# Sliding-window attention and RWKV channel mix: the first batch's q and k in half quads, its mask on PE, and batch 3's outputs turned by the crossbar

## The chip, the core and the metric

The kernel runs on one core of a Trainium2 chip. A core has TensorE (PE), VectorE (DVE), ScalarE (ACT), GpSimd (POOL) and SyncE (SP), each with its own in-order queue, and 16 DMA engines. SP and ACT issue transfers on hardware queues, POOL on a software queue that can also convert fp32 to bf16 on the way. The metric is the device time of one execution in microseconds (us), less is better.

## What is computed

```python
B, H, S, D = 8, 8, 576, 64; window = 128; scale = 1 / sqrt(D)
scores = scale * q @ k^T - slope[h] * (i - j)        # only 0 <= i - j < 128, else -1e9
attn = softmax(scores);  x = (attn @ v) as [B, S, H*D = 512]
x_prev = x shifted by one row of the sequence (zeros first)
xk = mu_k * x + (1 - mu_k) * x_prev;  xr = the same with mu_r
k = relu(xk @ w_k)            # 512 -> 1024
out = sigmoid(xr @ w_r) * ((k * k) @ w_v)             # 1024 -> 512
```

All inputs and the output are fp32 in DRAM. The kernel computes in bf16 with fp32 accumulation; the first half of the mix's gate is a tanh, with the factor folded into the relu.

## The kernel before

The kernel is a list of steps. Each step (`op`, `dma`, `pool_op`) names its engines, an estimated duration, the steps it depends on, a priority, and the buffers it takes and gives back (`Hold`). `Plan.run` simulates the engines with these estimates and so writes out a fixed order of instructions for each engine; the chip then runs these orders with semaphores between engines. A step's priority comes from `rank`, which adds the constants of `LEAD`, `SHIFT` and `NUDGE` (a number for each step by its index). A step that may run on two engines goes to one of them by the plan. All transfers of POOL are issued in the order of `LOADS` and then batch by batch.

Names of the trace: `qx` holds fp32 q and k of the first loads, `raw` q and k as loaded, `qt` and `qk` q and k with the head dimension on partitions, `at` the exponentials, `vs` and `tv` v with a column of ones, `xu` the normalised output of attention, `xt` that output transposed, `dl`, `xk`, `xr` the shift and its two mixes, `kk` the squared relu, `rs` the gate, `ot` the result. `duo` are two pairs of PSUM banks, `uno` four single ones.

*Batches 1 to 7.* Heads come in two quads of 4. `quad_load` (L559) brings a quad's q or k (576 rows) with 18 rows of 64 in each partition, 32 partitions a head. `turn` (L1145) transposes it on DVE (L1150), in 32 x 32 blocks, into `qt`. `scores4` (L1160) computes four heads at once, each on 32 rows of PE (two passes for 64), in two halves: `QUAD0` (k blocks 0 and 1 with q rows 0 to 384) and `QUAD1` (the rest), each 512 columns a head. ACT takes the exponentials of two heads at a time (L1190), and DVE multiplies them by a mask that holds the bias's exponential and the window (L1200). `attend` multiplies with v (L796) and normalises on DVE (L802, L807). `out_t` transposes on PE (L834) and copies on ACT (L710) for batches 1 to 3; for batches 4 to 7 (`XO`) `out_flip` uses a transposing DMA from SP (L882). `shift` makes xk and xr on DVE (L860, L867). `gate_load` puts a one-row copy on POOL's queue (L653) ahead of a batch's loads, for batches 6 and 7, that waits for the transposing DMAs of the batch two before.

*Batch 0* has a path of its own. Its rows 0 to 256 are loaded in fp32 by SP (q) and ACT (k), eight transfers of 128 KB (L574): two heads, two heads, then four. The first two pairs of heads are cast to bf16 on DVE and transposed on PE (L1091); the other two pairs are transposed in fp32 on PE (L1088). Copies by ACT or DVE put them into `qk`. Rows 256 to 512 come through POOL (L536) and are transposed on PE in 64 x 64 blocks (`qk_quad`, L1044), the last 64 rows apart (`tail_load` L554, `tails` L897). `scores` (two heads at a time on 64 rows of PE, L740) first writes the bias and the window by a matmul of scaled identity (`sid`) and distance (`dist`) into PSUM (L727), so that no mask is multiplied. Part 0 (rows 0 to 256) goes through to xk before part 1. The mask for the later batches is made by eight exponentials on ACT (L1130) that wait for part 0's last xk.

*Channel mix.* `channel_mix` takes a run of columns (256, 256, 384 and 256 columns for the first two batches, then 512, 384 and 256 for each pair): for each of 8 blocks four matmuls with w_k (L949), relu on ACT (L956), a square on ACT (L920) or DVE (L922); then for each 128 rows four matmuls with w_r (L967), tanh on ACT (L974), eight matmuls with w_v (L983), the product on DVE (L988) and a store by SP. Before the first data come, and in gaps, PE runs 90 matmuls on zeros (`warm`, L701).

POOL's order at the start is `LOADS = 'vK23tVkabRcWw'`: first half of batch 0's v, first half of w_k, run loads of rows 256 to 512 for the two quads, the tails, second half of v, second half of w_k, batch 1's q and k, w_r, batch 1's v, the halves of w_v.

```python
QUAD0 = (((0, 0, 256), (1, 128, 256)), 0)
QUAD1 = (((2, 256, 256), (3, 384, 192), (4, 512, 64)), 256)
PART = (((((0, 0, 256), (1, 128, 128)), 0),),
        ((((1, 256, 128), (2, 256, 256)), 128),
         (((3, 384, 128), (3, 512, 64), (4, 512, 64)), 512)))
```

Each triple is a block of 128 keys, the first query row and the number of queries.

Of the kernel before, what the change touches and what calls it, by code (L numbers as in the profile page):

```python
# [9 lines left out]
FP32 = mybir.dt.float32  # L10
# [172 lines left out]
def kernel(  # L183
# [30 lines left out]
    NQ, NA, NX, NV, NC, NT = 4, 4, 4, 2, 2, 3  # L214
    XO = range(4,B)
# [3 lines left out]
    NWARM = 90  # L219
    LOADS = 'vK23tVkabRcWw'  # L220
    XD = 4
    OTL = 3.5
    FIN = 384
    RATE = 284.0
    QUAD = 0.040
    RUN = {2: 64 * 284 / 345.0}
# [4 lines left out]
    FX = (0, 4, 4, 4, 4, 4, 0, 0)  # L231
# [3 lines left out]
    WAIT = 5.15  # L235
    COST = {'first': 1.28, 'v': 1.15, 'q': 0.944, 'ts': 0.66, 'tv': 0.58, 'w': 0.88, 'quad': 1.0, 'run2': 1.55, 'flip': 1.0, 'mu': 1.0, 'x': 1.0}

    def XU(b, g):
        return (DVE,)

    def SQ(order):
        return (DVE, ACT)

    XT0 = (ACT,)
    QK0 = (ACT, DVE)
    CAST = (DVE,)
    FT = (2, 3)
    KQ = ACT
    VCUT = True
    VDEP = 1  # L250
    TCOST = 1.5
    TURN = 0.42
    KLAST = 1

    def XT(b, g):
        return (ACT,) if b else XT0

# [3 lines left out]
    def many(n, shape, dtype, name):  # L261
# [5 lines left out]
    tv_buf = many(NV, [128, H, W], BF16, "tv")  # L267
    ts_buf = many(1, [128, H, D], BF16, "ts")
    tt_buf = many(1, [128, G, 3, 64], BF16, "tt")
    qk_buf = many(NQ, [128, 2, SM], BF16, "qk")  # L270
    qx_buf = cst.tile([128, 4096], BF16, name="qx")
    raw1 = raw_buf[1].rearrange("p i c x -> p (i c x)")
    half_buf = raw1[:, 0:4096].rearrange(
        "p (a i r h d) -> p a i r h d", a=2, i=2, r=2, d=D)
    part_buf = raw1[:, 2048:4096].rearrange(
        "p (i h r d) -> p i h r d", i=2, r=2, d=D)
    stage = qx_buf.bitcast(FP32).rearrange(
        "p (g i w) -> p g i w", i=2, g=4)
    at_buf = many(NA, [128, 2 * 1024 + 64], BF16, "at")
    rc_buf = many(NX, [128, 2, NJ], FP32, "rc")  # L280
# [12 lines left out]
    dist = cst.tile([128, 768], BF16, name="dist")  # L293
    sid = cst.tile([128, H, 128], BF16, name="sid")
    wk_sb = cst.tile([128, NPO, DF], BF16, name="wk_sb")
# [19 lines left out]
    plan = Plan(dict(p2=2, p1=N1, pt=4 - N1, qk=NQ, at=NA, xu=NX, vs=NV, cb=NC, qt=NT, ts=1, tt=1, xt=2, dl=2, dl0=4,  # L315
# [10 lines left out]
    def dve_t(n, fast=1):  # L326
# [4 lines left out]
        PE: (379.11, 948.28, 321.48, 777.92, 344.48, 715.92, 627.75, 578.6, 241.8, 354.15),  # L331
        ACT: (700.83, 2.12, 322.35, 108.16, 185.72, -3.46, 340.58, 397.46, 747.05, 580.68),
        DVE: (282.18, -111.4, 162.81, 61.6, 37.49, 18.01, -37.8, -38.84, 70.95, -86.71),
# [3 lines left out]
        PE: {(0, 0): -1189.02, (3, 0): 492.42, (2, 0): 367.63, (1, 0): 298.05, (1, 1): -728.2, (1, 2): 117.95, ('p1', 'fxk'): -1.92, ('rl', 'fp1'): -1166.05, ('frl',): 219.95, ('rs', 'fp1'): 514.38, ('p1', 'fkk'): 4.9, ('fkk',): 426.5, ('ot', 'fp1', 'frs'): 532.6, ('fp1', 'frs'): -626.2},  # L337
        ACT: {(0, 0): -688.81, (3, 0): -610.15, (2, 0): -722.11, (1, 0): 289.16, (1, 1): -432.67, (1, 2): 1038.71, ('p1', 'fxk'): 478.01, ('rl', 'fp1'): 76.23, ('frl',): 491.94, ('rs', 'fp1'): -82.07, ('p1', 'fkk'): -497.1, ('fkk',): 342.85, ('ot', 'fp1', 'frs'): -48.3, ('fp1', 'frs'): 278.04},
# [123 lines left out]
    def dma(queue, kb, issue, emit, deps=(), need=(), free=(), lat=(1.0, 0.9), flip=False, kind='x'):  # L462
# [809 lines left out]
```

## Time and profile before

| | us |
|---|---|
| median of 3 runs | 228.2 (227.05 to 228.41) |
| the profiled execution | 227.53 |
| its span | 225.8 |
| PE, DVE, ACT, POOL busy | 217.1, 196.3, 166.6, 59.7 |

In the profile "L949" is line 949 of the kernel before. A row of a group reads: line, engine, operation, out<-in with shapes, count, then busy us and mean ns of one, then idle time of the engine before these instructions and what ended it. A row of a timeline reads: start, length (several merged instructions may stand in one row), engine, line, operation, count, and in brackets the idle time before. Ends of matmuls are modelled and overlap the next one's start, so what a matmul occupies is read from start to start. A row of the chain reads start, length, what. Granted clock 1.00 is full speed of TensorE.

### The profile page before, as it was taken

What the parts mean: (1) busy time and instruction counts of PE and PEld (TensorE: products, weight loads), DVE (VectorE), ACT (ScalarE), POOL (GpSimd) and SP (SyncE); (2) the same over time, 40 slices, a digit from 0 to 9 for tenths busy, and PEclk for the clock granted to TensorE, in tenths of its full rate; (3) what the DMA queues carried; (4) which work ended last, traced back from release to release, by engine and by line L of the source; (5) the groups of instructions that cost most, each with busy time, mean ns of one, the idle gap of its engine ahead of it and who ended that gap; (6) DMA issues with size and microseconds to landing.
All of it is one profiled execution on the core that took longest, in us unless ns stands there. A gap on an engine that the chain in (4) does not pass through costs nothing.

```text
span 225.8 us, 5825 instructions
## 1 busy us (share of the span) xinstructions
PE 217.1 (96%) x2339; PEld 128.5 (57%) x2339; DVE 196.3 (87%) x386; ACT 166.6 (74%) x311; POOL 59.7 (26%) x88
## 2 busy tenths in 40 slices
PE   8999978999999999999999999999999999999993
PEld 8576636755756555554774546445674455456542
DVE  7388999999999999999999999999989966983332
ACT  3669999766999789978996796677996684427511
POOL 8776525465100910160007500091000000000000
PEclk9999999999999999999999999999999999999998
DMA  6999999999971997095434995489991315140023
GB/s 157 182 165 195 202 153 207 192 175 233 208 162 49 83 197 179 3 130 88 151 77 58 219 190 108 106 130 188 165 112 29 144 46 121 39 154 37 3 93 139
DMA packets 66298, 29.74 MB, mean 132 GB/s; under 512 B 53976, under 2 KB 58336, under 8 KB 66272
## 3 DMA queue, kind: packets, MB, share of 16 engines
q0 software_dynamic: 46832, 16.26, 66.9%
q1 hardware_dynamic: 17696, 12.53, 20.5%
q10 hardware_dynamic: 1744, 0.59, 1.0%
q8 instruction: 18, 0.29, 0.5%
q14 instruction: 8, 0.07, 0.1%
HBM read 33.56 MB, written 9.44 MB: 190 GB/s over the span
## 4 chain that ended last, share of the span: by engine, by line
PE 80%; DVE 8%; ACT 6%; DMA 3%; issue 1%; SPq 1%; DVEq 0%; ACTq 0%
PE uno L949 25%; PE uno L983 25%; PE uno L967 12%; PE duo L796 7%; PE duo L1173 6%; DMA qx<-in_q_dram 3%; DVE xu L807 2%; DVE qt L1150 2%; ACT at L1190 2%; PE uno L834 2%; PE uno L701 1%; DVE xk L867 1%; ACT mask L1130 1%; ACT at L754 1%; DVE xr L867 1%
## 5 line engine op out<-in xcount | busy, mean ns | idle before, releaser
L949 PE MATMUL uno<-xk,wk_sb 128*128 128x256 bf16 (+2 forms) x416 | 71.3, 314 | 1.7 <-DVE xk L867 1.3
L983 PE MATMUL uno<-wv_sb,kk 128*128 128x512 bf16 (+2 forms) x296 | 68.4, 374 | 0.0
L1190 ACT ACTIVATE at<-duo 128x1024 bf16<-128x1024 f32 x56 | 55.3, 1038 | 12.5 <-PE duo L1173 12.3
L956 ACT ACTIVATE rl<-uno 128x256 bf16<-128x256 f32 (+2 forms) x104 | 47.7, 483 | 14.1 <-PE uno L949 12.8
L949 PEld LDWEIGHTS <-wk_sb 128*128 128x128 bf16 x416 | 38.6, 98 | 24.1 <-issue 3.0
L983 PEld LDWEIGHTS <-kk 128*128 128x128 bf16 x296 | 27.2, 98 | 30.1 <-issue 1.9
L540 POOL DMA_DIRECT2D vs<-in_v_dram x32 | 28.5, 903 | 38.9 <-PE duo L796 29.9
L1200 DVE TENSOR_TENSOR at<-at,mask 128x1024 bf16<-128x1024 bf16 x56 | 37.1, 679 | 1.0 <-ACT at L1190 1.0
L967 PE MATMUL uno<-wr_sb,xr 128*128 128x512 bf16 x144 | 35.9, 379 | 0.0
L974 ACT ACTIVATE rs<-uno 128x512 bf16<-128x512 f32 x36 | 22.0, 618 | 18.5 <-PE uno L967 17.5
L920 ACT ACTIVATE kk<-rl 128x256 bf16<-128x256 bf16 (+2 forms) x67 | 33.7, 530 | 0.8
L1150 DVE STREAM_TRANSPOSE qt<-raw 128x576 f32<-128x576 f32 x28 | 33.7, 1233 | 0.0
L988 DVE SCALAR_TENSOR_TENSOR ot<-rs,uno 128x512 f32<-128x512 bf16 (+2 forms) x37 | 24.0, 663 | 6.7 <-ACT rs L974 4.6
L867 DVE SCALAR_TENSOR_TENSOR xr<-dl,mu_sb,xt 128x576 bf16<-128x576 bf16 (+1 forms) x32 | 24.6, 774 | 0.1
L867 DVE SCALAR_TENSOR_TENSOR xk<-dl,mu_sb,xt 128x576 bf16<-128x576 bf16 (+1 forms) x32 | 24.5, 774 | 0.0
L807 DVE TENSOR_TENSOR xu<-duo,rc 128x640 bf16<-128x640 f32 x28 | 22.8, 818 | 1.5 <-PE uno L834 0.8
L796 PEld LDWEIGHTS <-at 128*128 128x128 bf16 x576 | 21.6, 98 | 4.4 <-issue 0.3
L967 PEld LDWEIGHTS <-xr 128*128 128x128 bf16 x144 | 13.4, 98 | 13.6 <-issue 0.2
L922 DVE TENSOR_TENSOR kk<-rl 128x256 bf16<-128x256 bf16 (+2 forms) x37 | 12.2, 334 | 8.7 <-ACT rl L956 8.0
L796 PE MATMUL duo<-vs,at 128*128 128x65 bf16 x448 | 18.9, 193 | 0.0
L1173 PE MATMUL duo<-qt 32*128 32x256 bf16 (+2 forms) x560 | 18.0, 250 | 0.7 <-ACT at L1190 0.4
L1173 PEld LDWEIGHTS <-qt 32*128 32x128 bf16 x560 | 11.9, 92 | 11.5 <-issue 9.7
(73 smaller groups left out, 160.4 us busy)
## 6 DMA issues: line engine op xcount, KB each, us to landing
out_dram<-ot SPq DMA_DIRECT2D x34, 256.0 KB, 2.8
vs<-in_v_dram POOLq DMA_DIRECT2D x32, 128.0 KB, 10.0
raw<-in_q_dram POOLq DMA_DIRECT2D x14, 288.0 KB, 8.2
raw<-in_k_dram POOLq DMA_DIRECT2D x14, 288.0 KB, 9.3
wk_sb<-in_moe_w_k_dram POOLq DMA_DIRECT2D x2, 512.0 KB, 7.5
wv_sb<-in_moe_w_v_dram POOLq DMA_DIRECT2D x2, 512.0 KB, 11.5
qx<-in_k_dram ACTq DMA_DIRECT2D x4, 128.0 KB, 5.1
qx<-in_q_dram SPq DMA_DIRECT2D x4, 128.0 KB, 4.8
```

The lines of the kernel that those rows point to most:

```text
L540: return dma(POOL, 256, issue_t(1024), lambda e: nc.gpsimd.dma_start(out=vs_buf[h.idx][:, j, :, 0:D], in_=v[b, :, 128 * j:128 * j + 128].r ...
L796: nc.tensor.matmul(a[:, hl, t - t0], lhsT=at[:, lo:lo + 128], rhs=vs[:, u, 2 * g + hl, :] if u < NF else tvb[:, 2 * g + hl], start=(u == u ...
L867: lambda e: nc.vector.scalar_tensor_tensor(out=buf[hk.idx][:, g, e0 + c0:e0 + c1], in0=dls(), scalar=mu[:, g:g + 1], in1=xc(1), op0=ALU.mu ...
L920: nc.scalar.activation(out=out, in_=in_, func=AF.Square)
L949: nc.tensor.matmul(one(hp)[:, 0:n], lhsT=wk_sb[:, po, 128 * fo:128 * fo + 128], rhs=xk_buf[hx.idx][:, po, c0:c1], start=(po == 0), stop=(p ...
L956: a = op(ACT, act_t(n), [s], pr, lambda e, hp=hp, hr=hr: nc.scalar.activation(out=rl_buf[hr.idx][:, 0:n], in_=one(hp)[:, 0:n], func=AF.Rel ...
L967: nc.tensor.matmul(one(hp), lhsT=xr_buf[hx.idx][:, po, 128 * c:128 * c + 128], rhs=wr_sb[:, po], start=(po == 0), stop=(po == NPO - 1))
L983: nc.tensor.matmul(one(hv)[:, a:b], lhsT=kk_buf[hk.idx][:, fo, o:o + 128], rhs=wv_sb[:, fo, a:b], start=(fo == 0), stop=(fo == NFO - 1))
L1150: nc.vector.transpose(out=qt_buf[hq.idx][:, S * i:S * i + S].rearrange("p s t -> p (s t)").bitcast(FP32) .rearrange("p (q t) -> p t q", t=TB),
L1173: nc.tensor.matmul(two(hps[j // 2])[:, j % 2, c0:c0 + n], lhsT=qt[r:r + 32, S + 128 * u:S + 128 * u + 128, t], rhs=qt[r:r + 32, q0:q0 + n, t],
L1190: lambda e, ah=ah, j=j: nc.scalar.activation(out=ah(), in_=two(hps[j]), func=AF.Exp, scale=float(scale)), (), [hps[j]])
L1200: nc.vector.tensor_tensor(out=a, in0=a, in1=m, op=ALU.mult)
```

## The change

Batch 0 uses the quads' path of the other batches, in two halves of rows.

- The first half of each quad (k rows 0 to 256, q rows 0 to 384: what `QUAD0` needs) is loaded in fp32 in one transfer each, k by SP and q by ACT, into two `kk` buffers; a cast on ACT or DVE writes it as bf16 into `raw`. The rest (k 256 to 576, q 384 to 576) comes by POOL with conversion, four transfers.
- DVE transposes each half (`turn_half`), `scores4` computes it on 32 rows of PE. Bias and window of all four half scores of batch 0, and of the first half of quad 0 of batch 1, are written on PE (`emit_b`); those exponentials have no mask multiplication. The second quad's first half uses four single PSUM banks and four exponentials of 512 columns.
- The run loads, the tails, PE transposes of q and k with their copies, `scores`, and the wider part of `dist` are gone.
- The mask's exponentials wait for the fourth cast, in place of part 0's last xk.
- POOL's order: v, w_k first half, half loads, w_k second half, second half of v, batch 1's q and k, w_r, batch 1's v, w_v.
- Batch 3 joins batches 4 to 7 in the transposing DMA, and batch 5's loads get the gate.
- Squares of the first mix are on DVE alone; the normalising of batch 0's second part may go to ACT. Warm-up matmuls are 36. Buffers: `at` 5 (4), `vs` and `tv` 3 (2), `qt` 4 (3), `rc` 6 (4).
- `LEAD` is zero, `SHIFT` empty, `NUDGE` another table, `WAIT` 0: the order of all engines is a new one.

```diff
-    NQ, NA, NX, NV, NC, NT = 4, 4, 4, 2, 2, 3
-    XO = range(4,B)
+    NA, NX, NV, NC, NT = 5, 4, 3, 2, 4
+    XO = range(3,B)
...
-    NWARM = 90
-    LOADS = 'vK23tVkabRcWw'
+    NWARM = 36
+    LOADS = 'idvK34kVaRbcWw'
...
+    BIAS = ((0, 0, 0), (0, 0, 1), (0, 1, 0), (0, 1, 1), (1, 0, 0))
+    SINGLE = ((1, 0),)
...
-    FX = (0, 4, 4, 4, 4, 4, 0, 0)
+    FX = (0, 1, 1, 1, 1, 1, 0, 0)
...
     def XU(b, g):
+        if b == 0:
+            return (DVE, ACT)
         return (DVE,)
 
     def SQ(order):
-        return (DVE, ACT)
+        return (DVE, ACT) if order else (DVE,)
...
+    CAST = (ACT, DVE)
+    CUT = ((0, 384, 576), (0, 256, 576))
...
+    def half_load(i, c, t, h, g):
+        t0, r = CUT[i][t], CUT[i][t + 1] - CUT[i][t]
+        src = (q, k)[i][0, 4 * c:4 * c + 4, t0:t0 + r].rearrange("h (p r) d -> h p r d", p=32)
+        e0, e1 = t0 // 32 * D, (t0 + r) // 32 * D
+        return dma(POOL, HALFKB[r], issue_t(128), lambda e: nc.gpsimd.dma_start(
+            out=raw_buf[h.idx][:, i, c, e0:e1].rearrange("p (r d) -> p r d", d=D), in_=src), [g], kind="half")
...
+        for c in range(2):
+            for i in (1, 0):
+                r = CUT[i][1]
+                src = (q, k)[i][0, 4 * c:4 * c + 4, 0:r].rearrange("h (p r) d -> h p (r d)", p=32)
+                eng, e = (SPE, nc.sync) if i else (ACT, nc.scalar)
+                x = dma(eng, r * 1.024 * HWCOST, 0.46, lambda _, i=i, c=c, e=e, src=src: e.dma_start(
+                    out=stage(c, i), in_=src), [last["kk0"]], lat=(0.85, 0.75), kind="first")
+                cl[0][c, i, 0] = op(CAST, {ACT: act_t(r * 2, True), DVE: dve_t(r * 2)}, [x],
+                                    (0, 0, 0, 2 * c, 5), lambda e, i=i, c=c, r=r: copy_any(
+                    e, raw_buf[ch[0].idx][:, i, c, 0:2 * r], stage(c, i)), (), [hs[c]])
...
-    ms = [op(ACT, act_t(256, True), [n_dist] + gate, (2, h), lambda e, h=h: make_mask(h))
+    ms = [op(ACT, act_t(256, True), [n_dist, n_cast[3]], (2, h), lambda e, h=h: make_mask(h))
           for h in range(H)]
...
+        def emit_b(e):
+            for j in range(4):
+                for (u, q0, n) in pieces:
+                    c0 = BASE[u] + q0 - 128 * u - a0
+                    nc.tensor.matmul(
+                        bank(j)[:, c0:c0 + n], lhsT=sid[:, 4 * c + j],
+                        rhs=dist[:, 0:n], start=(u == pieces[0][0]), stop=False,
+                        skip_group_check=True)
...
-                            start=(t == 0), stop=(t == 1), skip_group_check=True)
+                            start=(t == 0 and not bias), stop=(t == 1), skip_group_check=True)
...
+            if bias:
+                res[p].append(x)
+                continue
...
+    def turn_half(c, t, hq, deps):
+
+        res, n = [], None
+        for i in (1, 0):
+            t0, w = CUT[i][t], CUT[i][t + 1] - CUT[i][t]
+
+            def emit(e, i=i, t0=t0, w=w):
+                nc.vector.transpose(
+                    out=qt_buf[hq.idx][:, S * i + t0:S * i + t0 + w].rearrange("p s t -> p (s t)")
+                    .bitcast(FP32).rearrange("p (q t) -> p t q", t=w // 32),
+                    in_=raw_buf[ch[0].idx][:, i, c, 2 * t0:2 * (t0 + w)].bitcast(FP32).rearrange(
+                        "p (t w) -> p t w", w=32))
...
+    for c in range(2):
+        hq = Hold("qt")
+        y = turn_half(c, 0, hq, [])
+        has = [Hold("at"), Hold("at")]
+        s0, m0 = scores4(0, c, 0, hq, has, y)
+        first.append((hq, y, has, s0, m0))
+        for j in range(2):
+            g = 2 * c + j
+            prio = (0, 0, 0, g)
+            r, hx = attend(0, g, 0, 2, has[j], m0[j] + vl[0][0:2], prio)
+            xks[0, 0, g], xrs[0, 0, g] = out_t(0, g, 0, 2, hx, [r], prio, xh[0], xth[0], late)
```

More of the change, by code (lines that the diff above doesn't have):

```diff
@@ new lines @@
+    s0.succ.append((n_mut, 0.0))
+    y[1].succ.append((n_mcopy[0], 0.0))
+    for n in (n_mut, n_mcopy[0]):
+        n.left += 1
+    for f in late:
+        xrs[0, 0, f.g] = f([xks[0, 0, G - 1]])
+    for c, (hq, y, has, s0, m0) in enumerate(first):
+        y = turn_half(c, 1, hq, [(x, 0.0) for x in y])
+        s1, m1 = scores4(0, c, 1, hq, has, y + [(s0, 0.0)])
+        for j in range(2):
+            g = 2 * c + j
+            prio = (0, 0, 1, g)
+            r, hx = attend(0, g, 2, NJ, has[j], m0[j] + m1[j] + vl[0] + blank, prio)
+            xks[0, 1, g], xrs[0, 1, g] = out_t(0, g, 2, NJ, hx, [r], prio, xh[0], xth[0])
```

409 lines of the change are left out of this document (106 added, 303 removed), and 143 rows, old and new, of the table NUDGE.

## The prediction

> **What bounds the kernel now.** I read the page's totals and slices first, then the table of stretches, then the chain in order of time, then the timelines of PE, DVE and ACT over the first 40 us.
>
> ```profile
> span 225.8 us, 5825 instructions
> ...
> PE 217.1 (96%) x2339; PEld 128.5 (57%) x2339; DVE 196.3 (87%) x386; ACT 166.6 (74%) x311; POOL 59.7 (26%) x88
> ...
> DVE  7388999999999999999999999999989966983332
> ...
> PE 80%; DVE 8%; ACT 6%; DMA 3%; issue 1%; SPq 1%; DVEq 0%; ACTq 0%
> ```
>
> PE is the bound as a whole, and DVE runs beside it nearly full until three quarters of the span. The stretches (us; then busy time of PE, PEld, DVE, ACT, POOL with counts; granted clock; DMA share; GB/s) show where this is not so:
>
> ```profile
> 17.00:27.00 10.00, 10.00 (x176) 6.85 (x174) 8.96 (x24) 9.91 (x26) 6.19 (x8) 1.00 1.25 199
> 27.00:36.00 9.00, 6.31 (x99) 3.83 (x100) 9.00 (x19) 8.66 (x16) 3.34 (x6) 1.00 2.06 170
> 36.00:60.00 24.00, 23.46 (x281) 15.24 (x274) 23.67 (x41) 19.14 (x41) 12.31 (x18) 1.00 1.58 203
> ...
> 100.00:140.00 40.00, 40.00 (x427) 22.74 (x425) 38.93 (x65) 33.70 (x60) 7.49 (x10) 1.00 0.83 128
> ```
>
> From 36 us on PE has almost no gap and DVE has 1.07 us free in 40. Before that three things change places: up to 17 us PE waits for data, from 17 to 27 PE and ACT are both full, and from 27 to 36 PE is idle 2.7 us (9.00 - 6.31) while DVE has not a moment free. The chain in order of time (start, length, what) says what the first 17 us are made of, and two PE lines where the first stage of the channel mix begins:
>
> ```profile
> 2.27 5.85 DMA qx<-in_q_dram
> ...
> 8.16 1.12 PE uno L1088 x7
> ...
> 15.29 1.19 ACT qk L710 x4
> 16.48 0.62 ACT mask L1130 x2
> ```
> ```profile
> 16.64 1.03 PE L949 MATMUL uno<-xk,wk_sb 128*128 128x256 bf16 x8 [0.37 <-DVE xk L867]
> ...
> 34.69 0.92 PE L949 MATMUL uno<-xk,wk_sb 128*128 128x256 bf16 x7 [0.41 <-DVE xk L867]
> ```
>
> So the last q of the first loads lands at 8.12 us (2.27 + 5.85), real mix work starts at 16.64, and at 34.69 PE still waits for DVE's xk of batch 0. After 36 us a saved us of PE work is worth a us only if DVE follows.
>
> **The change part by part.**
>
> *First loads (until the first mix).* Before, eight transfers of 128 KB bring 1.05 MB as 256 and 512 byte runs. After, four transfers bring 4 heads x 64 x 4 bytes x (256 + 384) rows x 2 quads = 1.31 MB in runs of 2 and 3 KB, k by SP and q by ACT. Their speed is not in this trace; the rows around it, us by us:
>
> ```profile
> 2.00:3.00 1.00, 1.00 (x13) 1.00 (x11) 1.00 (x9) 0.10 (x1) 1.00 (x2) 1.00 0.91 268
> 3.00:4.00 1.00, 1.00 (x12) 1.00 (x11) 1.00 (x6) 1.00 (x1) 1.00 (x2) 1.00 1.03 287
> ...
> 7.00:8.00 1.00, 0.61 (x7) 0.26 (x6) 0.24 (x4) 1.00 (x2) 1.00 (x3) 1.00 1.92 160
> ```
>
> At 287 GB/s, 1.31 MB from 2.0 us land at 6.6, 1.5 us earlier than 8.12; if the time per byte stays that of before, (8.12 - 2.0) x 1.25 = 7.65, they land at 9.65, 1.5 later. What follows also changes: fp32 transposes on PE (1.12 us) and a copy make room for casts on ACT or DVE and stream transposes on DVE. Rows for these:
>
> ```profile
> L1200 DVE TENSOR_TENSOR at<-at,mask 128x1024 bf16<-128x1024 bf16 x56 | 37.1, 679 | 1.0 <-ACT at L1190 1.0
> L1150 DVE STREAM_TRANSPOSE qt<-raw 128x576 f32<-128x576 f32 x28 | 33.7, 1233 | 0.0
> ...
> L922 DVE TENSOR_TENSOR kk<-rl 128x256 bf16<-128x256 bf16 x19 | 5.5, 288 | 2.5 <-ACT rl L956 2.0
> ...
> L807 DVE TENSOR_TENSOR xu<-uno,rc 128x384 bf16<-128x384 f32 x4 | 2.2, 553 | 0.0
> ...
> L710 DVE COPY qk<-uno 128x256 bf16<-128x256 bf16 x4 | 1.5, 416 | 0.0
> ...
> L710 DVE CAST tt<-uno 128x256 bf16<-128x256 f32 x2 | 0.8, 418 | 0.0
> L710 DVE CAST qk<-uno 128x512 bf16<-128x512 f32 x1 | 0.7, 692 | 1.7 <-PE uno L1088 1.7
> ```
>
> A quad's first half costs one cast after its last landing (0.7 to 1.0 us) and DVE transposes of 256 + 384 of 576 columns, 640/576 x 1.23 = 1.4 us. That is about 0.9 us more than the PE transposes and copy (1.12 + 0.69 = 1.8 against some 2.3 plus a wait), and the first quad's half is already through while the second lands. I take 0 for this part; bounds -1.5 (early landing) and +2.5 (late landing 1.5 and 1.0 of longer chain).
>
> *Batch 0 on PE, second part.* Removed from 15 to 26 us: 64 transposes of 64 rows (L1044), 12 pairs of bias and 64-row score matmuls with the tails (L727, L740, L897). Measured start to start on PE's timeline:
>
> ```profile
> 17.97 0.50 PE L727 MATMUL duo<-dist,sid 128*128 128x384 bf16 x2
> 18.40 0.34 PE L740 MATMUL duo<-qk 64*128 64x128 bf16 x4
> 18.67 0.34 PE L1044 MATMUL uno<-ident,raw 64*64 64x64 bf16 x16
> 18.95 0.61 PE L949 MATMUL uno<-xk,wk_sb 128*128 128x256 bf16 x4
> 19.39 0.38 PE L727 MATMUL duo<-dist,sid 128*128 128x256 bf16 x2
> ...
> 35.84 0.64 PE L1173 MATMUL duo<-qt 32*128 32x256 bf16 x24 [0.23 <-ACT at L1190]
> 36.41 1.48 PE L949 MATMUL uno<-xk,wk_sb 128*128 128x256 bf16 x12
> ```
>
> A wide bias pair and its scores take 0.43 + 0.27, a narrow one with tails about 0.32 + 0.22 by the same reading (some 0.11 per 256 columns), 16 transposes 0.28: four of each is 4 x 0.70 + 4 x 0.54 + 4 x 0.28 = 6.1 us. Added: two half scores of 32 rows at 0.57 (36.41 - 35.84) = 1.1, and two bias sets of 4 x 512 columns, 8 x 0.11 plus 0.1 for the switch, 2.0 in all. PE saves 3.0 us here, and pays 1.0 for the bias of batch 1's first half. Net 2.0.
>
> *ACT and DVE from 17 to 36 us.* PE's saving is covered by the other two engines, so these decide. ACT: the 8 mask exponentials (they stood at 16.3 to 22 and cost 0.31 each start to start, 0.62 for two) now wait only for a cast and can lie in ACT's idle first 15 us: -2.5; its squares of the first mix go to DVE, its qk copies (1.19 for four) are gone. ACT stops being a limit. DVE: -4 x 0.416 = -1.7 for qk copies, -0.8 for tt, +2.2 for four half transposes (320 + 192 columns, twice: 1024/576 x 1.233), +1.2 for four more squares (4 x 0.288; I count half of the eight as already there), -1.4 for two mask multiplications of batch 1 (2 x 0.679); xu of the second part may go to ACT, 0 to -2.2 (4 x 0.553). Sum -0.5 to -2.7. DVE was busy 8.96 + 9.00 = 17.96 of these 19 us, so the stretch can shrink to 17.5 or 15.3: 1.5 to 3.7 us. PE allows it: 10.00 + 6.31 - 2.0 = 14.3. I take 2.0, near the lower end, as moving xu is only an option and DVE also has to wait for its inputs.
>
> *Loads by GpSimd.* Four half loads replace four run loads and two tail loads, and the second half of wk goes ahead of v's second half. The queue was the pace for batch 1, whose last k is what GpSimd's next issue waited for:
>
> ```profile
> 27.53 0.74 POOL L565 DMA_DIRECT2D wv_sb<-in_moe_w_v_dram  x1 [0.59 <-DMA raw<-in_k_dram]
> ```
>
> It carries 4 x 128 + 2 x 64 = 640 KB before and 512 after, so batch 1 lands some 0.8 us earlier (128 KB of its own at 170 GB/s), and v's second half about as late as before or up to 3 us later, behind 512 KB more. I price both at 0: the attention that needs v is paced by DVE. If v is later than DVE, it costs up to 3.
>
> *Batch 3 by the crossbar.* Removed: 20 PE transposes and 4 ACT copies. Added: 4 issues on SP, ahead of output stores, and a gate on POOL ahead of batch 5's loads.
>
> ```profile
> 46.16 0.72 PE L834 MATMUL uno<-ident,xu 128*128 128x128 bf16 x10
> 46.72 1.03 PE L983 MATMUL uno<-wv_sb,kk 128*128 128x512 bf16 x4
> ...
> L710 ACT COPY xt<-uno 128x576 bf16<-128x576 bf16 x12 | 7.8, 661 | 1.5 <-PE uno L834 1.5
> ...
> L860 DVE TENSOR_TENSOR dl<-xt 128x576 bf16<-128x576 bf16 x28 | 12.3, 446 | 1.9 <-DMA xt<-xu 1.9
> ...
> xt<-xu SPq DMA_TRANSPOSE x16, 2.7
> ...
> L653 POOL COPY gap<-xt 1x4 bf16<-1x4 bf16 x2 | 1.5, 750 | 39.1 <-ACT at L1190 20.3 <-DMA xt<-xu 18.8
> ```
>
> PE saves 20 x 0.056 = 1.1 us ((46.72 - 46.16)/10), ACT 4 x 0.66 = 2.6. DVE's 16 dl behind a crossbar transfer lost 1.9 us, 0.12 each, so four more cost 0.5 at worst. The SP issue hides behind six output buffers; POOL idles some 20 us at each gate already. DVE has 1 us free in 40 and ACT room to take squares off it, so I take -1.0; bounds -1.1 and +0.5.
>
> *Order.* The tables that rank instructions are replaced whole, so every engine's order from 36 us on is new, with the same work in it. No row shows the new order; I take 0, and as bounds the 2.7 us that PE stands idle from 27 to 36, either way. Warm-up matmuls fall from 90 to 36: they fill gaps, 0.
>
> Sum: 227.53 (the profiled execution's time, its span 225.8 and 1.7 around it) - 2.0 - 1.0 = 224.5. The median of the runs shown is 228.2, 0.7 above the profiled one, so 225.2 us on its scale, 1.3% less.
>
> **The rivals.**
>
> A, slower: the first loads land late. Mechanism: both quads' fp32 halves (25% more bytes) share the DMA engines with v and wk from 2.2 us on, and the second q carries a cast and two DVE transposes behind it. For it: DMA throughput fell from 287 to 160 GB/s once GpSimd's loads ran. Against it: longer runs. At the upper bounds, first loads +2.5 with nothing regained later by DVE and batch 3 at +0.5 gives 227.5 + 3.0 + 0.7 = 231.2. It decides from a last landing of about 9.5 us on, and shows in a first L949 after 19 us.
>
> B, no gain: DVE stays the bound and nothing is regained. Removed PE and ACT work turns into idle time in 17 to 36 us, because half transposes and squares fill DVE again, and PE's 1.1 us of batch 3 becomes waiting for DVE. For it: DVE at 9.00 of 9.00 and 38.93 of 40. Against: ACT's relief lets it take squares and xu. Time: 228.2 less 0.0 to 1.0, say 227.7.
>
> C, the clock. The trace shows the first warm matmuls at 0.11 us apart and later ones at 0.055:
>
> ```profile
> 0.99 3.38 PE L701 MATMUL uno<-warm 128*128 128x128 bf16 x30 [0.99 <-DVE warm L504]
> ...
> 11.58 1.05 PE L701 MATMUL uno<-warm 128*128 128x128 bf16 x16
> ```
>
> With 36 of them spent at the start, PE may idle between 8 and 16 us and run at half pace again when the mix starts. If 3.4 us (the length of the slow start here) run at half pace, 1.7 us are lost: 225.2 + 1.7 = 226.9. The Trainium skill, "TensorE: Matmul & The Clock Gate", section "Part 1: The HAM clock gate", speaks against the change here: it says the array falls back to half clock after an idle window of about 3.4 us and needs as long of work to recover. The trace agrees on the ramp (0.11 us, then half); no gap of such length is in it to show the fall. Bias matmuls need only dist and sid and break up the gap, so I give it little.
>
> **How the numbers follow.** The forecast (a gain of 1 to 7 us about 225.2; its own range 221.5 to 227) has 0.54, of which 0.44 lies under 225.9, 1% below the median, about what a measurement here can tell from no change. A has 0.22, B 0.16, C 0.08 (a third of C, without the other losses, would still be faster). Faster: 0.44 + 0.03 = 0.47. Slower by over 1% (above 230.5): A's late half and a bad order with it, 0.24 with the forecast's and B's upper tails. Within: 0.29. The range for 8 in 10 runs from 221.3 (DVE's 3.7, batch 3's 1.1 and some of the order's 2.7 gained) to 231.2 (A).
>
> **What would show it.** Right: last q of the first loads landed before 8.5 us; first L949 at 16 to 17 us; PE's busy time between 17 and 36 with less than 1 us idle and the second part's xk done before 32 us instead of 35; no L834 for batch 3, and L860 waits under 3 us in all. Wrong: first L949 after 18 us (A), DVE without gap and PE idle over 2 us in 17 to 36 (B), L949 at 0.21 us apart in the first mix (C), or PE idle in the steady stretch, which would be the order.

## Result and the profile after

| | before | after |
|---|---|---|
| median, us (4 runs each) | 227.62 (226.94 to 228.41) | 242.27 (242.00 to 242.65) |
| ratio, 95% interval | | 1.064 (1.060 to 1.068) |
| span of the profiled execution | 225.8 | 240.2 |
| mean granted clock | 0.997 | 0.941 |

The change makes the kernel 14.7 us slower, outside the range given, on rival A's side. Lines L842, L858, L824, L967 and L990 of the new kernel are the old L967, L983, L949, L1173 and L1190. The page's totals, slices and chain:

```profile
span 240.2 us, 5571 instructions
...
PE 212.3 (88%) x2188; PEld 127.0 (53%) x2217; DVE 192.0 (80%) x378; ACT 169.3 (71%) x322; POOL 58.2 (24%) x87
...
DVE  4014498999999999979999999979998997964132
...
PEclk9855558999999999999999999999999999999999
...
PE 68%; DVE 13%; DMA 12%; issue 3%; ACT 2%; SPq 0%; DVEq 0%; ACTq 0%
```

PE, DVE and ACT together have about as much work as before (573.6 us against 580.0), but the second digit of DVE is 0, the clock is at half from the third slice to the sixth, and DMA holds 12% of the chain where it held 3%. The stretches that the prediction showed:

```profile
17.00:27.00 10.00, 3.88 (x44) 2.43 (x44) 4.27 (x14) 5.43 (x12) 2.48 (x3) 0.50 0.65 86
27.00:36.00 9.00, 7.32 (x105) 5.91 (x106) 7.24 (x24) 5.70 (x12) 5.59 (x9) 0.50 0.99 143
36.00:60.00 24.00, 21.57 (x298) 15.64 (x299) 22.66 (x50) 21.33 (x55) 11.01 (x16) 0.96 1.74 174
100.00:140.00 40.00, 39.04 (x407) 22.28 (x410) 38.37 (x69) 31.38 (x59) 8.89 (x14) 1.00 0.80 118
```

From 17 to 27 us PE works 3.88 of 10 us instead of all of them. The chain in order of time, and then ACT and PE on the timeline, name the reason:

```profile
0.74 0.74 SPq L563
1.54 19.78 DMA kk<-in_k_dram
...
21.86 1.94 ACT at L990 x2
23.85 1.86 PE duo L955 x12
```
```profile
16.20 1.35 ACT L571 CAST raw<-kk 128x512 bf16<-128x512 f32 x2 [12.43 <-DMA kk<-in_k_dram]
...
18.49 1.04 PE L967 MATMUL duo<-qt 32*128 32x256 bf16 x16 [12.27 <-DVE qt L1017]
...
21.34 0.62 ACT L571 CAST raw<-kk 128x512 bf16<-128x512 f32 x1 [3.78 <-DMA kk<-in_k_dram]
...
25.64 1.04 PE L967 MATMUL uno<-qt 32*128 32x256 bf16 x16
...
39.93 0.60 PE L824 MATMUL uno<-xk,wk_sb 128*128 128x256 bf16 x4 [0.56 <-ACT xu L712]
```

The second quad's k, whose issue follows the first quad's at 1.48 us (0.74 + 0.74), is there at 21.3 (1.54 + 19.78). The last first load landed at 8.12 before. PE waits 12.27 us for the first quad, and the second quad's first scores start at 25.64; the kernel before started its last scores of part 0 at 10.74:

```profile
10.74 0.34 PE L740 MATMUL duo<-qk 64*128 64x256 bf16 x4
```

The first mix starts at 39.93 instead of 16.64. That is 23.3 us later, more than the whole loss, because the new order also puts more work ahead of it, such as the scores of both second halves: 14.3 us lie between the second quad's first scores and the first mix (39.93 - 25.64), where 5.9 lay before (16.64 - 10.74).

The transfers of the first 4 us, in the view of the DMA queues, after and then before (packets, MB, the time that the packets took as a share of 16 engines):

```profile
DMA packets 31, 0.10 MB, mean 24 GB/s; under 512 B 0, under 2 KB 0, under 8 KB 31
...
q10 hardware_dynamic: 31, 0.10, 10.2%
```
```profile
DMA packets 1290, 0.58 MB, mean 144 GB/s; under 512 B 266, under 2 KB 1290, under 8 KB 1290
...
q1 hardware_dynamic: 720, 0.31, 27.4%
q10 hardware_dynamic: 570, 0.27, 22.8%
```

With nothing else on the queues, the longer runs move 0.10 MB where the short ones moved 0.58. The transfers begin at 2.2 us in the one and at 1.8 in the other, so 10.2% of 16 engines' 4 us is 3.6 packets at a time while they run, and 50.2% (27.4 + 22.8) is 14.6. So the loads are slow from their first microsecond, before GpSimd's transfers can be in their way.

### The profile page after: what moved, and what is told of

It reads as the page before. It is cut to its first block, busy times and chain, and to the rows that moved or that the text cites. A ratio compares the mean times of both kernels' runs of the same rounds, so it can differ in the third digit from the quotient of the medians.

```text
span 240.2 us, 5571 instructions
## 1 busy us (share of the span) xinstructions
PE 212.3 (88%) x2188; PEld 127.0 (53%) x2217; DVE 192.0 (80%) x378; ACT 169.3 (71%) x322; POOL 58.2 (24%) x87
## 4 chain that ended last, share of the span: by engine, by line
PE 68%; DVE 13%; DMA 12%; issue 3%; ACT 2%; SPq 0%; DVEq 0%; ACTq 0%
PE uno L858 22%; PE uno L824 19%; PE uno L842 10%; DMA kk<-in_k_dram 8%; PE duo L967 6%; PE duo L694 5%; DVE qt L929 4%; DMA xt<-xu 3%; PE duo L955 2%; DVE at L1004 2%; PE uno L733 2%; ACT at L990 2%; DVE xu L706 1%; PE uno L694 1%; DVE xr L766 1%
## 5 line engine op out<-in xcount | busy, mean ns | idle before, releaser
L990 ACT ACTIVATE at<-duo 128x1024 bf16<-128x1024 f32 x62 | 61.6, 1030 | 17.7 <-PE duo L967 17.4
L824 PE MATMUL uno<-xk,wk_sb 128*128 128x256 bf16 (+2 forms) x410 | 71.1, 313 | 0.8 <-ACT xu L712 0.6
L858 PE MATMUL uno<-wv_sb,kk 128*128 128x512 bf16 (+2 forms) x286 | 67.0, 373 | 0.7 <-issue 0.3
L831 ACT ACTIVATE rl<-uno 128x256 bf16<-128x256 f32 (+2 forms) x104 | 46.4, 476 | 12.0 <-PE uno L824 8.5
L824 PEld LDWEIGHTS <-wk_sb 128*128 128x128 bf16 x416 | 38.7, 98 | 23.5 <-issue 2.1
L858 PEld LDWEIGHTS <-kk 128*128 128x128 bf16 x296 | 27.6, 98 | 30.6 <-issue 1.2
L1004 DVE TENSOR_TENSOR at<-at,mask 128x1024 bf16<-128x1024 bf16 x54 | 35.9, 682 | 0.6 <-ACT at L990 0.6
L842 PE MATMUL uno<-wr_sb,xr 128*128 128x512 bf16 x131 | 35.2, 379 | 0.9 <-issue 0.2
L795 ACT ACTIVATE kk<-rl 128x256 bf16<-128x256 bf16 (+2 forms) x70 | 35.0, 519 | 1.1
L863 DVE SCALAR_TENSOR_TENSOR ot<-rs,uno 128x512 f32<-128x512 bf16 (+2 forms) x37 | 24.4, 664 | 13.3 <-PE uno L858 11.1
L967 PE MATMUL duo<-qt 32*128 32x256 bf16 (+2 forms) x624 | 21.2, 260 | 14.2 <-DVE qt L1017 12.3
L849 ACT ACTIVATE rs<-uno 128x512 bf16<-128x512 f32 x36 | 21.1, 601 | 15.3 <-PE uno L842 12.2
L967 PEld LDWEIGHTS <-qt 32*128 32x128 bf16 x640 | 14.7, 96 | 25.9 <-issue 12.4
L842 PEld LDWEIGHTS <-xr 128*128 128x128 bf16 x144 | 13.3, 98 | 14.3 <-issue 0.8
L694 PE MATMUL duo<-vs,at 128*128 128x65 bf16 x448 | 18.2, 194 | 1.3 <-ACT at L990 1.3
L621 POOL COPY gap<-xt 1x4 bf16<-1x4 bf16 x3 | 1.6, 536 | 69.4 <-DMA xt<-xu 36.5
```

The lines of the kernel that those rows point to most:

```text
L694: nc.tensor.matmul(a[:, hl, t - t0], lhsT=at[:, lo:lo + 128], rhs=vs[:, u, 2 * g + hl, :] if u < NF else tvb[:, 2 * g + hl], start=(u == u ...
L795: nc.scalar.activation(out=out, in_=in_, func=AF.Square)
L824: nc.tensor.matmul(one(hp)[:, 0:n], lhsT=wk_sb[:, po, 128 * fo:128 * fo + 128], rhs=xk_buf[hx.idx][:, po, c0:c1], start=(po == 0), stop=(p ...
L831: a = op(ACT, act_t(n), [s], pr, lambda e, hp=hp, hr=hr: nc.scalar.activation(out=rl_buf[hr.idx][:, 0:n], in_=one(hp)[:, 0:n], func=AF.Rel ...
L842: nc.tensor.matmul(one(hp), lhsT=xr_buf[hx.idx][:, po, 128 * c:128 * c + 128], rhs=wr_sb[:, po], start=(po == 0), stop=(po == NPO - 1))
L858: nc.tensor.matmul(one(hv)[:, a:b], lhsT=kk_buf[hk.idx][:, fo, o:o + 128], rhs=wv_sb[:, fo, a:b], start=(fo == 0), stop=(fo == NFO - 1))
```

## Experiments

**Theory F, fan-out.** The new transfers have the pattern "h p (r d)", four heads outermost, and are spread over four DMA engines; the old ones had 128 partitions outermost and used sixteen. The Trainium skill, "DMA: Bandwidth & Descriptors", section "Why a DMA increments its semaphore by 16 and not by 1", states this rule: the number of engines is the largest up to 16 that divides the outermost dimension (leaving out those of size 1) of both sides; the same page's section "Rules for kernel authors" advises a multiple of 16 there. It spoke against this change, and the prediction overlooked it. **Rivals:** Q, GpSimd's loads crowd the first ones out on the queues (rival A's mechanism); C, the half clock costs the time; O, the new order or batch 3's crossbar. The experiments run on the changed kernel unless they say "before".

**e1: sixteen engines.** Each first half goes as four transfers of one head, 32 partitions outermost (the code here and below is shortened):

```diff
-e.dma_start(out=stage(c, i), in_=src)          # "h p (r d)"
+for h in range(4):
+    e.dma_start(out=stage(c, i)[32 * h:32 * h + 32],
+                in_=(q, k)[i][0, 4 * c + h, 0:r].rearrange("(p r) d -> p (r d)", p=32))
```

> The changed kernel, but each fp32 first half is issued as four transfers of one head (32 partitions each) in place of one transfer of four heads; the plan and every engine's order stay as they are. Theory F (fan-out): one transfer whose DRAM side counts 4 heads first is spread over only four DMA engines, as the first 2 us of ACT's queue suggest (31 packets of 3 KB, about four at a time); 32 partitions a transfer use all. Then the first cast starts before 6.5 us (16.2 in the changed kernel), the fourth before 10 (22.5), the first L949-type mix matmul before 20 us (39.9), no half clock after 12 us, and the time is 225 to 230 us. Rival Q (contention): the fp32 halves starve because GpSimd's packets take turns with them on all engines; then four transfers change nothing: first cast after 12 us, time above 237 us. Rival S (order): the new order loses in the steady part; then the first mix comes early but the time stays above 233 us.

Measured: 233.55 us, ratio 1.0245 (1.0220 to 1.0269). The issues, the casts and the scores of the two quads:

```profile
0.74 7.66 ACTq L565 DMA_DIRECT2D kk<-in_q_dram  x8
...
9.79 2.02 ACT L575 CAST raw<-kk 128x512 bf16<-128x512 f32 x3
12.08 1.04 PE L971 MATMUL duo<-qt 32*128 32x256 bf16 x16 [4.29 <-DVE qt L1021]
14.46 0.56 DVE L575 CAST raw<-kk 128x768 bf16<-128x768 f32 x1 [1.97 <-DMA kk<-in_q_dram]
16.96 1.04 PE L971 MATMUL uno<-qt 32*128 32x256 bf16 x16
```

The second quad's scores start 8.7 us earlier than in the changed kernel (16.96 against 25.64), and the time falls by 8.7 us. So the pattern of these transfers costs 8.7 us, as F has it. But I expected 225 to 230 us, with the fourth cast before 10 us: 5.6 us of the loss remain (233.55 - 227.94), ACT spends until 8.4 us on issuing eight transfers, and the fourth cast starts at 14.46. GpSimd's bf16 halves, issued at the same times in both kernels, land 11.0 to 11.5 us after their issue instead of 22.6 to 23.1, so the four-engine transfers had held up these as well.

**e2: GpSimd's half loads as single heads too** (e1, plus four transfers for each of their four).

> As the run before, and GpSimd's four half loads are also issued as four transfers of one head each (16 issues in place of 4). Theory F: if these too ran on four engines, they land within 8 us of their issue instead of over 20, and the time falls a further 0 to 2 us; against it GpSimd's queue issues 12 more transfers, about 0.5 us each, ahead of w_k's second half and v, so up to 3 us could be lost there. Rival Q: no change from the run before in landing times.

233.26 us, 1.0242 (1.0214 to 1.0271): no different from e1. These transfers land 2.9 to 4.7 us after their issue, but the last of them is issued at about 17 us instead of 7. So the gain in e1 is that of the hardware queues' loads; what the fan-out of GpSimd's own is worth, this run does not separate from its later issues.

**e4 and e7: the same on the kernel before.** Each of its eight first loads is cut in two, 124 and 4 partitions (e4) or 64 and 64 (e7), so that both have 16 issues and the same bytes, and differ in where they are cut and so in what divides the outermost dimension (by F 124 and 4 get four engines, 64 sixteen).

```diff
-qe.dma_start(out=dst, in_=src)
+for lo, hi in ((0, 124), (124, 128)):      # e7: ((0, 64), (64, 128))
+    qe.dma_start(out=dst[lo:hi], in_=src[lo:hi])
```

> The kernel before, with each of its eight fp32 first loads issued as two transfers, of 124 partitions and of 4. Theory F: 124 partitions divide over four engines only, so these loads of the same bytes and runs become as slow as the changed kernel's: the first cast moves from 3.3 us to after 6, the last q lands after 13 us instead of 8.1, and the time rises by 4 to 12 us; of this the eight additional issues explain at most 2 us. Rival Q: the split changes nothing but the issues: time up by less than 2 us.

> The kernel before with each first load issued as two transfers of 64 partitions: the same 16 issues as in the run with 124 and 4 partitions, which took 250.9 us, but both shares divide over sixteen engines. Theory F: the loads land about as fast as before, and the time is 227.5 to 231 us; the rest is the price of eight more issues. Rival (the additional issues, not the fan-out, made 250.9): above 240 us.

e4: 250.94 us, 1.1011 (1.0984 to 1.1039). e7: 236.63 us, 1.0329 (1.0267 to 1.0392). SP's issues and PE's first mix, of e4 and then e7, and SP's issues in the kernel before:

```profile
0.75 21.57 SPq L576 DMA_DIRECT2D qx<-in_q_dram  x8
...
40.44 1.03 PE L952 MATMUL uno<-xk,wk_sb 128*128 128x256 bf16 x8 [0.37 <-DVE xk L870]
```
```profile
0.74 7.32 SPq L576 DMA_DIRECT2D qx<-in_q_dram  x8
...
24.35 1.03 PE L952 MATMUL uno<-xk,wk_sb 128*128 128x256 bf16 x8 [0.37 <-DVE xk L870]
```
```profile
0.74 2.03 SPq L574 DMA_DIRECT2D qx<-in_q_dram  x4
```

The fan-out alone is worth 14.3 us (250.94 - 236.63; 15.6 by the two ratios) in a kernel that has nothing else of the change. Cutting each load in two, eight more issues of the same bytes, costs some 8 us as well: SP's issues take 7.32 us instead of 2.03, and the first mix comes at 24.35 instead of 16.64. Both times lie above what I expected, as I had given these issues 2 us at most.

**e12, e11, e10: the crowding.** Two columns of the second quad's staged k and q are copied on GpSimd ahead of one of its loads, so that this and all later ones wait until the fp32 halves have landed: ahead of v on the changed kernel (e12) and on e5 below (e11), ahead of the first half of w_k on e5 (e10).

```diff
+for i in range(2):
+    nc.gpsimd.tensor_copy(out=hold_sb[:, i:i + 1], in_=stage(1, i)[:, 0:1])
 nc.gpsimd.dma_start(out=vs_buf[h.idx][:, j, :, 0:D], ...)
```

> The changed kernel with its four single transfers, and GpSimd's loads (v and all after) held until they have landed, so that nothing shares the DMA engines with them. Theory F: on four engines of about 18 GB/s each (3 KB in 0.169 us), 1.31 MB need some 18 us even alone; the first cast starts after 8 us and the fourth after 17 us, and the time is 242 to 250 us. Rival Q (contention alone made them late): they land by 7 us, the first cast starts before 5.5 us and the time falls below 234 us.

243.16 us, 1.0671 (1.0612 to 1.0731). The queues from 4 to 10 us, where nothing but the first loads runs, and the casts:

```profile
DMA packets 229, 0.59 MB, mean 98 GB/s; under 512 B 4, under 2 KB 4, under 8 KB 229
...
q10 hardware_dynamic: 127, 0.38, 16.5%
q1 hardware_dynamic: 102, 0.21, 9.0%
```
```profile
12.30 1.35 ACT L584 CAST raw<-kk 128x512 bf16<-128x512 f32 x2 [8.51 <-DMA kk<-in_k_dram]
16.96 0.62 ACT L584 CAST raw<-kk 128x512 bf16<-128x512 f32 x1 [3.31 <-DMA kk<-in_k_dram]
```

16.5 + 9.0 = 25.5% of 16 engines is 4.1 packets at a time for the two queues together, so four engines, and 98 GB/s with the queues to themselves. That agrees with the Trainium skill's rule above. In the changed kernel, with GpSimd's transfers beside them, the same queues in the same 6 us:

```profile
q10 hardware_dynamic: 96, 0.29, 17.5%
q1 hardware_dynamic: 65, 0.13, 8.2%
```

They hold 25.7% there, again 4.1 packets at a time, and move 0.42 MB instead of 0.59. So crowding makes each packet slower and leaves their number at four. The last k still lands at 17.0, against 21.3 with the others beside it. So crowding is some 4 us of the delay and the fan-out the rest, and what is gained by holding GpSimd back is paid again when its loads come later (PE waits 5.94 us at 30.74, before the next scores). Q falls as the main cause.

**e5, e6: a free ACT, a warm PE.** e5 is e1 with the second quad's q issued by SP (12 issues) instead of ACT (4 left). e6 adds 39 matmuls on zeros to e5's warm-up.

> The run with one transfer a head, but the second quad's q is issued by SP too: SP issues twelve, ACT four. In the run before, ACT's first cast stood behind its eight issues (until 8.4 us) and its table load (8.49 to 9.77 us), though k had landed. Theory F with this addition: ACT is free by 3 us, loads its table, and the first cast starts between 4.5 and 6 us in place of 9.8; the chain behind it moves with it as far as the second quad's landing lets it, and the time falls by 2 to 5 us from 233.5, to 228 to 231. Rival Q (the halves starve beside GpSimd's transfers): the first cast stays after 8 us, no fall above 1 us. Rival S (the new order itself loses): the cast comes early, and the time stays above 232 us.

> As the run with SP's twelve issues, with 39 more warm-up matmuls in the last warm-up step (at about 4 to 8 us). If PE's idle time before the first scores costs its clock, the granted clock in the profile stays 1.00 from 8 to 27 us and the time falls by 0.5 to 3 us; if PE is not the limit there, or the first scores come early enough to hold the clock without this, within 0.5 us of the run without it.

e5: 234.14 us, 1.0247 (1.0193 to 1.0300); e6: 234.43 us, 1.0262 (1.0238 to 1.0285). In e5 the first cast starts at 7.1 instead of 9.8, yet the second quad's k lands at 13.3, and nothing is won (I expected 228 to 231). In e6 the clock fell again from 13 us on, so it says nothing on the clock.

> The same, with GpSimd's wait ahead of v too. The second quad's cast starts at 7.5 to 9 us. v then lands some 5 us later than before its wait (at 14 to 16 us): if v is not needed before the second quad's exponentials are done, 227 to 230 us; if it is, no better than the run with the wait ahead of w_k.

> As the run with SP's twelve issues, and GpSimd copies two columns of the second quad's staged k and q before it issues w_k, so its loads after v wait until the first loads have landed. In the runs so far the span less the start of the second quad's first scores was 214.6 (changed kernel), 214.2, 214.3 and 214.1 us: what comes late there comes late at the end. Theory F with contention as its second half: single-head transfers issued after 4 us land in 6 to 8 us because GpSimd's packets take turns with them; without w_k and the half loads beside them the second quad's cast starts at 8 to 10 us (13.4), its scores at 12 to 14 (17.8), and the time falls to 228 to 231 us, unless the half loads, now issued some 4 us later, become the next wait (then their transposes start after 21 us and the time stays above 232). Rival (issue time alone sets the second quad): the cast stays after 12 us.

e11: 234.28 us, 1.0276 (1.0227 to 1.0325); e10: 233.89 us, 1.0263 (1.0213 to 1.0314). The chain and two PE rows of e11:

```profile
6.19 1.92 DMA kk<-in_k_dram
...
8.80 1.92 POOL vs L520 x2
10.72 0.73 POOL wk_sb L537
11.45 10.01 DMA raw<-in_k_dram
```
```profile
12.69 1.04 PE L984 MATMUL uno<-qt 32*128 32x256 bf16 x16
...
22.62 1.04 PE L984 MATMUL duo<-qt 32*128 32x256 bf16 x24 [6.25 <-DVE rc L717]
```

Alone on sixteen engines the last k lands at 8.1 us (6.19 + 1.92) and the second quad's scores start at 12.69. But the bf16 halves, held back, land at 21.5, and PE waits 6.25 us there. In e10, between the two, these scores start at 15.01. Whichever goes first, the other is late, and neither run comes to the 227 to 231 us of the hopeful branch of its expectation; e10's had named the late halves as the other branch.

**e3, e13, e14, e15: the clock.** e3 runs 230 matmuls on zeros ahead of the first scores. e13 (on e5) and e14 (on e3) also fill the wait behind the first quad's scores, by matmuls that add zero to a bank of the second quad's bias; e15 does so on e10.

```diff
+for _ in range(95):                        # e14: 75, e15: 50
+    nc.tensor.matmul(spare[0](0)[:, 0:128], lhsT=warm, rhs=warm, start=False, stop=False, ...)
```

> The changed kernel with its single transfers, but the last warm-up step issues 230 matmuls on zeros in place of one, so that PE stays busy from about 4 to 18 us and keeps its full clock. Theory F: landing times stay (first cast at 16 us); only PE work between 18 and 37 us gets faster, some 5 to 6 us of busy time of which PE is not always the limit: 238 to 241 us against 242.3. Rival C (the clock is the cause): most of the loss of 14.6 us comes back, under 233 us.

> The kernel e5 (each first half as four single-head transfers, second quad's q issued by SP) with 95 more matmuls on zeros on PE right after the first quad's first-half scores: they add zero to a PSUM bank of the second quad's bias, so the result is unchanged, and they fill the 5.87 us in which PE waits there. In e5 the granted clock is 0.50 from 11 to 27 us, and the chain of waits holds 8.8 us of PE pieces in that stretch. Theory (half clock is the larger part of the 5.8 us that e5 still loses to the kernel before): the clock reads 1.00 until about 20 us, the second quad's scores take half as long, the first mix (32.04 us in e5) starts 2 to 4 us earlier, time 230 to 232. Rival (the rest is the later landing of the loads, and the clock lies beside it): first mix within 1 us of 32, time 233.3 to 235.

> The changed kernel with e3's 230 matmuls on zeros ahead of the first scores and 75 more behind the first quad's scores, where PE waits 3.55 us for the second quad's load in e3. In e3 the clock fell from 22 us on all the same, so e3 tested only a part of the clock's share. If the clock is worth several us, 237.5 to 240 (e3: 241.6); if only the loads count, 241 to 242.5.

> The kernel e10 (e5 with GpSimd's loads behind v held until the second quad's fp32 halves have landed) with 50 matmuls on zeros behind the first quad's scores. e10 took 233.9 us, with its second quad's scores at 15.01 us and the clock at half from 10 us on. If the clock is the larger part of the rest, 229.5 to 232; if the held loads pay it back later, 233 to 234.5.

| | us | ratio, 95% interval | mean clock |
|---|---|---|---|
| e3 | 241.60 | 1.0593 (1.0561 to 1.0624) | 0.969 |
| e14 | 240.77 | 1.0570 (1.0533 to 1.0608) | 0.984 |
| e13 | 232.76 | 1.0209 (1.0181 to 1.0237) | 0.993 |
| e15 | 234.16 | 1.0269 (1.0236 to 1.0303) | 0.971 |

The stretch from 11 us on and the second quad's scores in e13, with e5's row of the second stretch last:

```profile
11.00:17.00 6.00, 4.96 (x87) 4.81 (x85) 2.33 (x10) 3.01 (x6) 1.46 (x2) 1.00 1.32 185
17.00:27.00 10.00, 7.38 (x135) 5.61 (x134) 7.28 (x26) 7.37 (x18) 7.07 (x10) 0.83 1.59 183
```
```profile
17.47 0.63 PE L976 MATMUL uno<-qt 32*128 32x256 bf16 x16
...
31.03 0.60 PE L828 MATMUL uno<-xk,wk_sb 128*128 128x256 bf16 x4 [0.72 <-ACT xu L716]
```
```profile
17.00:27.00 10.00, 8.00 (x103) 5.82 (x105) 6.13 (x20) 6.51 (x15) 7.12 (x10) 0.50 1.53 187
```

With the clock up for most of the stretch (it reads 0.50 again from 23 to 26 us in e13), the time falls by 1.4 us (e13 against e5) and 1.5 (e14 against the changed kernel), or by 0.9 and 1.6 when the ratios are compared. That is near the scatter, as e5's four runs lie between 232.59 and 235.51. The traces agree in size: the first mix of e13 starts 1.0 us before that of e5 (31.03 against 32.04). It is less than the 2 to 4 that I expected for the clock as the larger part; that the 8.8 us of PE pieces at half pace are mostly bridged by waits that end where they did would explain it, and is not shown. In e3 the clock fell again from 22 us on, and the time by 0.7. In e15 the gain is gone, as PE waits for the held loads. The half clock is real and minor.

**e9: batch 3 by the crossbar alone, on before.** The transposing DMA is issued where PE's transposes stood, with every engine's order as it was; PE's 20 transposes and ACT's four copies are left out.

> The kernel before with one part of the change alone: batch 3's outputs go through the crossbar, issued by SP where PE's transposes stood, and PE's 20 transposes and ACT's 4 copies are left out; every other instruction keeps its place. My prediction's term: PE saves 1.1 us, so the time falls by about 1 us if DVE does not wait; the rival that DVE waits for four landings of 2.7 us at places that were chosen for 1 us: DVE idle before batch 3's differences rises by up to 1.7 us each, and the time rises by 0 to 4 us.

241.45 us, 1.0576 (1.0545 to 1.0607). Waits of PE, then of DVE, in e9:

```profile
PE duo L1178 <- DVE xu L807: 8.7, 4, 4.1
```
```profile
DVE xu L807 <- DMA xt<-xu: 10.7, 4, 5.0
```

In the old order DVE's next xu waits for the transposing DMA that reads xu's buffer, 10.7 us in all (0.5 in the kernel before), and PE behind it. The 13 us are far above both what my term said (1 less) and the rival (up to 4 more). The changed kernel has an order made for the crossbar: there DVE waits 2.6 us on this and 2.2 for dl, and in e13 0.2 and 0.3. So e9 prices the step in the wrong place: these long waits are not in the change, and what the step gains there no run shows.

**e8: the mask on PE undone.** On e6, batch 1's first half gets its mask from DVE again and no bias from PE.

> The run with SP's twelve issues and the longer warm-up (234.4 us), with batch 1's first half without the bias on PE: the mask is multiplied on DVE as in the kernel before (2 x 0.68 us), right before the second half's. My prediction's price: PE gains 1.0 us, DVE loses 1.4; DVE is full there, so the time rises by 0.5 to 1.5 us. Rival: neither is the limit after the late start: within 0.4 us.

235.87 us, 1.0342 (1.0290 to 1.0394), 1.4 us more than e6. That part of the change gains a little, about the 0.5 to 1.5 that was expected.

## Why the prediction was wrong

*The step that failed is "First loads", taken as 0 with bounds of -1.5 and +2.5.* It measured about +13 in the last landing (21.3 against 8.12) and about +14 in the end. Both bounds carried over a speed of the old transfers, 287 GB/s or their time per byte, and so assumed that a transfer of 384 KB in 3 KB runs uses as many DMA engines as one of 128 KB in short runs. It did not: 31 packets in 4 us against 1290. The upper bound was also the nearest row's, not a row of a transfer of this shape; the text said that their speed is not in the trace, and then left no room for that.

On sixteen engines and undisturbed, the loads land where the term had them, at 8.1 us for the last k (e11, between 6.6 and 9.65). What it also missed is that this cannot be had without a price here: four issues for each transfer on busy queues (e7: eight more cost 8 us in the kernel before), or the other loads later (e10, e11).

The delay passes to the end one to one. From the start of the first mix to the end of the span it is 200.3 us in the changed kernel (240.2 - 39.93) and 199.3 to 200.3 in all twelve runs on it (199.9 in e1 and in e11), so what sets their times lies ahead of the first mix. From the start of the second quad's first-half scores to the end it is 214.6 us in the changed kernel (240.2 - 25.64), 214.2 in e1 (231.2 - 16.96), 214.1 in e5 (231.8 - 17.75) and 213.0 in e13 (230.5 - 17.47); only where GpSimd's loads were held back it is longer, 216.0 to 219.8 in e10, e11, e12 and e15. The same difference of the kernel before, from its last scores of part 0, is 215.1 (225.8 - 10.74). So behind the first loads the changed kernel is 0.5 to 2.1 us quicker, where I forecast 3; that is argued from the spans, as no run had its second quad's scores before 12 us and all loads in time.

In spans the loss is 14.4 us (240.2 - 225.8): 13.2 in the last landing, 1.7 between it and the second quad's scores (4.3 us, 25.64 - 21.3, against 2.6, 10.74 - 8.12), and 0.5 less behind them. For the 1.7 the prediction had 0.9 (0.5 by its own 2.3 against 1.8, the rest a wait that no row shows), taken as 0 since "the first quad's half is already through while the second lands". It is not. In ACT's new order the cast of the second quad's k stands ahead of the first quad's exponentials, and a set of bias matmuls of PE waits for these: the chain above runs from the cast at 21.34 through the exponentials (21.86) and the bias (23.85) to the scores. In e13 the first quad's scores start at 9.40 and their exponentials at 14.51, after the second k has landed. No run changed this order, so what it costs stays open, and that part of rival O with it.

The sign of success, a first mix at 16 to 17 us, was read off the old order. With 14.3 us of work between the second quad's scores and the first mix, the new one could not show it even with the loads in time.

*Rival A* named the place and the sign: it had the loads late, decided from 9.5 us on, with a first mix after 19 us. Its cause was Q, bytes and crowding, and its price 3 us instead of 14, since it was worked out from the same bounds. *Rival C* came true as a consequence: PE idles from 6.2 to 18.5 us, and the clock reads 0.50 from 11 to 37 us. The Trainium skill, "TensorE: Matmul & The Clock Gate", section "Part 1: The HAM clock gate", has this fall after an idle window. This trace now shows it: the clock reads 1.00 until 10 us and 0.50 from 11 us on. The runs e13 and e14 price it at 0.9 to 1.6 us (forecast 1.7). *Rival B* was not tested: DVE never became the bound of these first 36 us.

*The other terms.* Batch 0 on PE, and ACT and DVE from 17 to 36 us: the gain of 2.0 can't be read in the stretch named, as PE idles in it; it lies in the 0.5 to 2.1 us above, with the order and batch 3. The mask's exponentials did not find an idle ACT: in e13 six of them stand in the chain, 1.75 us at 16.44. They wait for the fourth cast, and in ACT's order they stand ahead of the second quad's exponentials. Batch 3: -1.0 is not contradicted (its waits in e13 are 0.5 us) and not shown by itself. Loads by GpSimd, taken as 0: the bf16 halves landed 22.6 to 23.1 us after their issue in the changed kernel, and v's first ones after 19.4 (6.5 before), beside the slow loads. Order, 0: from 100 to 140 us PE is busy 39.04 of 40 us instead of 40.00, and 39.6 in e13, a loss of 0.4 to 1.0 in this stretch, within the bounds given. Warm-up, 0: 0.9 to 1.6 us by the clock, when the wait is that long.

Shares of the 14.7 us, on the changed kernel: 8.7 go with the fan-out undone by single-head transfers, 1.4 more with the clock (e13 ends 9.5 below the changed kernel, e5's queue choice costing 0.6, within the scatter). The last 4.6 us (232.76 - 228.18, the kernel before beside e13; it was 227.62 beside the changed kernel, hence 0.5 less in all) are argued from the trace of e13: its second quad's k lands 5.8 us later than the last load of before (13.9 against 8.12), the scores follow it after 3.6 us instead of 2.6, and the rest is 2.1 us shorter. The later landing goes with the sixteen issues and the crowding, which these runs do not divide further. A transfer of a whole quad with the 32 partitions of a head outermost would keep four issues and might get sixteen engines, but it would have to step partitions in a later dimension of the on-chip side; it was not tried. The Trainium skill, "DMA: Bandwidth & Descriptors", section "Rules for kernel authors", has such a transfer put its data at wrong addresses. No version tried beats the kernel before.

## What to carry to other kernels

Before pricing a load by bytes, look at the outermost dimension of both its sides: if it is not a multiple of 16 (4 or 124 here), price the load at the engines it gets (here four, 98 GB/s undisturbed). A bound for a cost that no row shows must vary what the rows have in common, here the number of engines, and not only their figures. And splitting a transfer to get the engines is not free either while the queues are full.

## What the runs showed that was not expected

- The rows fit an engine that keeps an issue until its queue has room. SP's eight issues took 21.57 us in e4 and 7.32 in e7, where four took 2.03 in the kernel before; on ACT the casts and exponentials behind such an issue wait too (7.66 us in e1).
- Larger runs are not faster by themselves: 3 KB packets at four engines moved 0.10 MB in the first 4 us, 256 and 512 byte packets at sixteen moved 0.58.
- A transposing DMA put in the place of a transpose on PE, with the order unchanged, cost 13 us through the buffer it reads (e9), while in an order made for it DVE waits 0.5 us in all on such transfers (e13).
